# Inner blocks in pairs, a ring of four banks, and a regrouped background turn in a fused attention, Fourier and MLP kernel

## The chip, the core and the metric

The kernel runs on one core of a Trainium2 chip. Its time is the device time of one launch in microseconds (us), the median over runs. Engines are named as the profile names them: PE (matrix multiply, with its weight loads as PEld), DVE (vector), ACT (scalar, activation functions), POOL and SP (which issues nearly all DMAs here). Each engine works through its own instructions in the order of the program; semaphores hold an instruction until what it reads is written and the buffer that it writes is free.

## What is computed

Three stages follow each other on a tensor of 4 batches, 768 positions and 384 channels (8 heads of 48).

```
for t in range(S):                       # gated linear attention, per batch and head
    state = alpha[t][:, None] * state + outer(k[t], v[t])
    y[t] = q[t] @ state
X = fft(fft(x, axis=1), axis=2); u = x + real(X)
un = (u - mean(u)) / sqrt(var(u) + 1e-6)
x = u + relu(un @ w_ch1) @ w_ch2         # 384 -> 1536 -> 384
gate = sigmoid(causal_conv5(x))          # per channel
out = (gate * (x @ w_val)) @ w_out
```

All is float32. The kernel keeps that precision by splitting operands into a high and a low part, so that one product becomes three matmuls (`mm3`).

## The kernel before

**Pieces.** The positions of a batch are cut into three pieces of 256, twelve in all. For each piece `mlp` runs twelve inner blocks of 128 hidden channels. A block is nine matmuls with `w1` into a bank of PSUM (`mm`), a relu on ACT that writes the high part (`hh`, L663), a DVE instruction that writes the low part (`hlo`, L665), and, two blocks later, nine matmuls with `w2` into `ch`. `mlp` is a generator: after each half block it yields, and the loop in `run` then makes one tick. A piece has 24 ticks.

**What a tick adds.** Each tick advances the side jobs by one step: `norm` of the next piece (mean, variance, the split into `hl`), `gate` of the previous piece (`L697`, the convolution `L716`, three products `va` with L736, two products `po` with L749/L752, the output DMA), in the first two pieces a conversion of weights on DVE (L221, L224, L228 and the low part L237), and from the second piece on `check`, which streams the inputs once more through SBUF and two activations on ACT (L134, L140 to L146). It also advances the background by a number of steps that `PACE` sets.

**The background.** While batch b goes through its pieces, `back` runs attention and the Fourier transform of batch b+1. Attention is done in 6 tiles of 128 positions, in turns: `attn_a` (two scans on DVE, L287 and L294, and the scaled k and q, L292 and L297), `attn_b` (transposes L309 with a copy on ACT, L310; scores L317 with the mask on DVE, L318), `attn_d` (output, L365 and L371, copied out by ACT, L376 to L378) and `attn_c` (products L334 and the state updates on DVE, L345 and L350). A turn works on up to three tiles at once: b, c of tile g-1, a of tile g, d of tile g-2. Each `yield` ends a step.

**The head.** Batch 0 has nothing to hide behind: `first` runs its attention by the strings in `FIRST`, one for each turn, in which letters stand for the parts above, `w` for a part of a weight conversion and `l` for up to four weight loads. Conversions work on two weights at a time where two are loaded.

**Banks.** PSUM has eight banks. Before, `mm` is a ring of three, shared by the inner blocks and by `gate`'s `va` and `po`; `aux` is a ring of three, for attention, the Fourier transform and `norm`; `ch0` and `ch1` hold the sums of `mlp`. A ring hands out its banks in turn, and the next user waits until the one before has been read.

Of the kernel before, what the change touches and what calls it, by code (L numbers as in the profile page):

```python
# [30 lines left out]
N_CHECK = 1152  # L31
N_FLAGS = 32
CHECK_FROM = 1
CHECK_STEP = 8
# [29 lines left out]
class Main:  # L64
# [14 lines left out]
    def aux(self):  # L79
        return self.t([P, 512], "aux", 3, pool=self.ps)  # L80

    def mm(self):
        return self.t([P, 512], "mm", 3, pool=self.ps)


    def constants(self):
# [9 lines left out]
        self.ends = cp.tile([P, A_W - 1], F32, name="ends")  # L96
# [108 lines left out]
    def weight_parts(self, count=2):  # L205
# [28 lines left out]
        for hi, lo, t, r, h, l in self.halves:  # L234
            if h is not None:
# [4 lines left out]
                rest = self.t([P, 512], "ch1" if self.pa else f"ch{self.n_rest % 2}", 1, pool=self.ps)  # L240
# [188 lines left out]
    def attention(self, b):  # L429
        g0 = b * NT  # L430
        for i in range(NT + 2):
            g = g0 + i
            if 1 <= i <= NT:
                yield from self.attn_b(g - 1)
            if i < NT:
                yield from self.attn_a(g)
                yield
            if i >= 2:
                yield from self.attn_d(g - 2)
                yield  # L440
            if 1 <= i <= NT:
                self.load_va(g - 1)
            if 1 <= i <= NT:
                yield from self.attn_c(g - 1)
                if i < NT:
                    self.load_v(g)
            if i + 2 < NT:
                self.load_qka(g + 2)
            if 1 <= i <= NT:
                yield  # L450
            if i == 0:
                for _ in range(LAG_BG):
                    yield
# [44 lines left out]
    def dft_part(self, t):  # L498

        if t == 0:  # L500
            self.pa = [self.mm() for _ in range(3)] + [self.t([P, 512], "ch0", 1, pool=self.ps)]
# [148 lines left out]
    def mlp(self, b, p):  # L650
        nc = self.nc
        uh, ul = self.nm[(b, p)][:2]
        hq = {}
        ch = None
        lag = 2
# [465 lines left out]
```

## Time and profile before

| | |
|---|---|
| runs | 659.2, 659.37, 660.25 us; median 659.37 |
| profiled execution | 657.75 us, span 655.9 us |
| head, up to the first inner block | 84 us |
| twelve pieces | 84 to 632 us |
| tail, the last gate | 632 to 656 us |

The profile is of one execution. A row of a group gives the number of its instructions, their busy time and mean length, and then the engine's idle time just before them and who ended it. The length of a matmul in the profile holds its way through the array; how fast PE goes is read from one start to the next.

### The profile page before, as it was taken

Reading aid. Unit: us, or ns where it says so; the run is one execution under the profiler, and the core shown is the slowest. Engines: PE = TensorE matmul, PEld = TensorE weight load, DVE = VectorE, ACT = ScalarE, POOL = GpSimd, SP = SyncE. Lnnn points to the kernel's source line nnn. Section 1 sums busy time; section 2 is a strip of 40 time slices with the busy share of each in tenths; the row PEclk is TensorE's granted clock in tenths of the full one; section 3 lists DMA queues with packets and bytes.
Section 4 is the critical chain, followed back from the end, with each engine's and each line's share of the span. In section 5 each row is a group of like instructions: output and inputs, shape, how many; then the busy total and the mean of one; then the engine's idle time right before and its main releaser. Section 6 shows DMA issues by size and latency. Waiting matters only on the chain.

```text
span 655.9 us, 15998 instructions
## 1 busy us (share of the span) xinstructions
PE 584.9 (89%) x6617; PEld 549.0 (84%) x6617; DVE 438.8 (67%) x1026; ACT 247.7 (38%) x609; POOL 157.3 (24%) x332
## 2 busy tenths in 40 slices
PE   3768996785998999899999999899999998999983
PEld 2557686775997899798999899898998998999973
DVE  7988689879747667857763958669365454454552
ACT  2333432322544453353353354343343433433231
POOL 0011023140316042132322322232231222322220
PEclk9986997698898999999999999999899999999996
DMA  9595044354255136335235247135052041310100
GB/s 337 180 343 179 20 175 81 94 136 158 61 171 104 44 120 148 123 122 83 62 135 106 86 131 183 35 135 118 26 128 74 14 88 42 73 34 26 9 25 30
DMA packets 27587, 69.50 MB, mean 106 GB/s; under 512 B 4976, under 2 KB 15728, under 8 KB 27504
## 3 DMA queue, kind: packets, MB, share of 16 engines
q1 hardware_dynamic: 27504, 68.38, 37.3%
q8 instruction: 54, 0.88, 0.6%
q14 instruction: 29, 0.24, 0.1%
HBM read 63.64 MB, written 4.73 MB: 104 GB/s over the span
## 4 chain that ended last, share of the span: by engine, by line
PE 67%; DVE 21%; DMA 4%; ACT 3%; issue 2%; POOL 1%; SPq 0%; DVEq 0%; POOLq 0%; ACTq 0%
PE mm L646 8%; PE mm L648 7%; PE mm L647 7%; PE ch L646 7%; PE ch L648 6%; PE ch L647 6%; PE mm L749 5%; PE aux L509 4%; PE aux L554 3%; PE aux L317 3%; DVE w L294 2%; DVE ga L716 2%; PE aux L365 2%; DVE hlo L665 2%; DVE w L287 2%
## 5 line engine op out<-in xcount | busy, mean ns | idle before, releaser
L665 DVE SCALAR_TENSOR_TENSOR hlo<-mm,hh 128x256 fp32r<-128x256 f32 x144 | 60.5, 420 | 121.1 <-ACT hh L663 120.7
L646 PE MATMUL mm<-hl,w1h 128*128 128x256 f32 x432 | 131.5, 304 | 4.4 <-DVE hlo L665 3.4
L646 PE MATMUL ch<-hh,w2h 128*128 128x256 f32 x432 | 129.5, 300 | 2.7 <-DVE ga L697 2.7
L647 PE MATMUL ch<-hh,w2l 128*128 128x256 f32 x432 | 122.9, 284 | 0.0
L648 PE MATMUL ch<-hlo,w2h 128*128 128x256 f32 x432 | 122.8, 284 | 0.0
L648 PE MATMUL mm<-hl,w1h 128*128 128x256 f32 x432 | 122.6, 284 | 0.0
L647 PE MATMUL mm<-hl,w1l 128*128 128x256 f32 x432 | 122.6, 284 | 0.0
L663 ACT ACTIVATE hh<-mm 128x256 fp32r<-128x256 f32 x144 | 54.2, 378 | 94.7 <-PE mm L648 94.0
L646 PEld LDWEIGHTS mm<-hl,w1h 128*128 128x128 f32 x432 | 83.2, 193 | 7.9 <-DVE hlo L665 4.2
L646 PEld LDWEIGHTS ch<-hh,w2h 128*128 128x128 f32 x432 | 82.7, 191 | 5.5 <-DVE ga L697 3.1
L647 PEld LDWEIGHTS mm<-hl,w1l 128*128 128x128 f32 x432 | 83.3, 193 | 0.8
L647 PEld LDWEIGHTS ch<-hh,w2l 128*128 128x128 f32 x432 | 82.8, 192 | 0.7
L648 PEld LDWEIGHTS mm<-hl,w1h 128*128 128x128 f32 x432 | 83.1, 192 | 0.2 <-DVE hl L606 0.2
L648 PEld LDWEIGHTS ch<-hlo,w2h 128*128 128x128 f32 x432 | 82.9, 192 | 0.0
L716 DVE SCALAR_TENSOR_TENSOR ga<-u,cw,ga 128x256 f32<-128x256 f32 x132 | 60.8, 517 | 0.0
L738 POOL TENSOR_TENSOR hl<-ga,hl 128x256 fp32r<-128x256 f32 x33 | 27.8, 845 | 105.8 <-ACT hl L737 105.8
L379 POOL COPY x<-x 128x1 f32<-128x1 f32 x24 | 12.3, 513 | 139.2 <-ACT x L376 121.5
L317 PEld LDWEIGHTS aux<-w 48*64 48x64 f32 x768 | 27.3, 148 | 14.5 <-DVE st L350 8.0
L317 PE MATMUL aux<-w 48*64 48x64 f32 x768 | 30.8, 236 | 9.7 <-DVE st L350 7.4
L749 PE MATMUL mm<-wvo,hl 128*128 128x384 f32 x198 | 38.1, 336 | 0.0
L612 POOL TENSOR_TENSOR tmp<-tmp,tmp 128x256 f32<-128x256 f32 x24 | 17.7, 737 | 74.0 <-ACT tmp L611 73.1
L749 PEld LDWEIGHTS mm<-wvo,hl 128*128 128x128 f32 x198 | 33.5, 188 | 0.0
(167 smaller groups left out, 1149.4 us busy)
## 6 DMA issues: line engine op xcount, KB each, us to landing
qka<-in_qka_dram SPq DMA_DIRECT2D x23, 772.5 KB, 5.3
ck<-in_w_dram SPq DMA_DIRECT2D x16, 576.0 KB, 4.8
vu<-in_vu_dram SPq DMA_DIRECT2D x24, 192.0 KB, 3.5
u<-in_w_dram SPq DMA_DIRECT2D x12, 384.0 KB, 4.9
va<-in_va_dram SPq DMA_DIRECT2D x24, 192.0 KB, 4.0
ck<-in_al_dram SPq DMA_DIRECT2D x8, 576.0 KB, 4.4
out_dram<-ga SPq DMA_DIRECT2D x24, 192.0 KB, 1.9
w<-in_cs_dram SPq DMA_DIRECT2D x6, 579.0 KB, 5.4
```

The costliest lines, as they stand in the source:

```text
L317: nc.tensor.matmul(out=sc[j * 64 : j * 64 + 64, cs], lhsT=kt[hs, cs], rhs=qt[hs, cs], start=True, stop=True)
L509: self.nc.tensor.matmul(out=pa[: d1 - d0, g * 193 : g * 193 + n], lhsT=self.eo[g][:, t, m, d0:d1], rhs=self.cs[g][:, t, m, :n], start=t == ...
L554: nc.tensor.matmul(out=pa[:, :385], lhsT=self.cd[:w, dt, mi, kt * P : (kt + 1) * P], rhs=pq[:w, mi, dt, :], start=dt == 0, stop=dt == 1)
L612: nc.gpsimd.tensor_tensor(out=ss, in0=ss, in1=sq, op=ALU.add)
L646: nc.tensor.matmul(out=out, lhsT=w[0][:, k, cols], rhs=xh, start=first, stop=False)
L647: nc.tensor.matmul(out=out, lhsT=w[1][:, k, cols], rhs=xh, start=False, stop=False)
L648: nc.tensor.matmul(out=out, lhsT=w[0][:, k, cols], rhs=xl, start=False, stop=last)
L663: nc.scalar.activation(out=hh, in_=hp[:, :NK], func=AF.Relu)
L665: nc.vector.scalar_tensor_tensor(out=hl, in0=hp[:, :NK], scalar=0.0, in1=hh.bitcast(F32), op0=ALU.max, op1=ALU.subtract)
L716: nc.vector.scalar_tensor_tensor(out=gs[:, j], in0=xs, scalar=w, in1=gs[:, j], op0=ALU.mult, op1=ALU.add)
L738: nc.gpsimd.tensor_tensor(out=gl[:, j], in0=gs[:, j], in1=gh[:, j].bitcast(F32), op=ALU.subtract)
L749: nc.tensor.matmul(out=po[:, :DM], lhsT=lh[:, k, ts], rhs=rh[:, k, :], start=n == 0, stop=n == 8)
```

## The change

Inner blocks are made in pairs: two blocks share one bank (2 x 256 columns), one relu and one DVE instruction of 512 columns serve both, and the `w2` products follow one pair later. The ticks stay 24 for a piece. `mm` becomes a ring of two banks for the inner blocks alone, `aux` a ring of four, and `va` and `po` move to `aux`. The background's turn is written as a string, `ORDER`, with a dot for the end of a step: transposes with scores (`Bb`), both scans at once (`Aa`), an empty step, the output with the scaled q (`Dt`), then products with the states' updates in the same step (`Cvc`). `FIRST` loads weights earlier. `check` takes smaller portions more often (768 columns, a period of 5 ticks, not 1152 and 8). A constant is held in bf16, and some lags and paces change.

```diff
-N_CHECK = 1152
+N_CHECK = 768
-CHECK_STEP = 8
+CHECK_STEP = 5
-BG_FROM = 6
-LAG_US = 5
+BG_FROM = 5
+LAG_US = 6
-LAG_RS = 2
-FIRST = ("Aqwwlwl", "aBwAqUwwSv", "BAwDwUaqvSw", "wBAwwwaDlwUvSq", "AlyllDBwUSavx", "BwAlDUlSawwwv", "aBwDlU0Sw1lf", "lgDwp2hr")
-PACE = (1, 0.8, 0.95, 1.05, 0.9, 0.95, 0.95, 0.9, 1, 1, 1, 1)
+LAG_RS = 3
+FIRST = ("Alwwlqwwl", "BlaAlUwqwSvl", "lBDAwwllUaqvlSw", "BwlwwAwDallwUvSq", "AllylDBwUSavx", "BwAlDUSlawwv", "BawDlU0lSww1lfl", "lDg2wpllrh")
+ORDER = "Bb.Aa..Dt.m.Cvc.q."
+PACE = (1, 0.8, 0.95, 1.15, 0.85, 0.85, 0.95, 0.95, 1, 1, 1, 1)
...
     def aux(self):
-        return self.t([P, 512], "aux", 3, pool=self.ps)
+        return self.t([P, 512], "aux", 4, pool=self.ps)
...
     def mm(self):
-        return self.t([P, 512], "mm", 3, pool=self.ps)
+        return self.t([P, 512], "mm", 2, pool=self.ps)
...
+            for what in ORDER:
+                if what in "Aat" and now:
+                    next(pa, None)
+                elif what in "Bb" and before:
+                    next(pb)
+                elif what in "Cc" and before:
+                    next(pc)
+                elif what == "D" and two:
+                    for _ in self.attn_d(g - 2):
+                        pass
...
+                elif what == ".":
+                    yield
...
-        for f in range(NF + lag):
+        for f in range(0, NF + 2, 2):
+            now = hq
             if f < NF:
                 hp = self.mm()
-                for k in range(KD):
-                    self.mm3(hp[:, :NK], self.w1, slice(f * P, (f + 1) * P), (uh[:, k], ul[:, k]), k, k == 0, k == KD - 1)
-                hh = self.t([P, NK], "hh", 3, F32R)
-                nc.scalar.activation(out=hh, in_=hp[:, :NK], func=AF.Relu)
-                hl = self.t([P, NK], "hlo", 3, F32R)
-                nc.vector.scalar_tensor_tensor(out=hl, in0=hp[:, :NK], scalar=0.0, in1=hh.bitcast(F32),
+                for i in range(2):
+                    cols = slice((f + i) * P, (f + i + 1) * P)
+                    for k in range(KD):
+                        self.mm3(hp[:, i * NK : (i + 1) * NK], self.w1, cols, (uh[:, k], ul[:, k]), k, k == 0, k == KD - 1)
+                    if i == 0:
+                        yield
+                hh = self.t([P, 2 * NK], "hh", 2, F32R)
+                nc.scalar.activation(out=hh, in_=hp, func=AF.Relu)
+                hl = self.t([P, 2 * NK], "hlo", 2, F32R)
+                nc.vector.scalar_tensor_tensor(out=hl, in0=hp, scalar=0.0, in1=hh.bitcast(F32),
                                                op0=ALU.max, op1=ALU.subtract)
...
-            va = self.mm()
+            va = self.aux()
...
-            po = self.mm()
+            po = self.aux()
```

Two places show how instructions move. The first is DVE in the first inner blocks of piece 0 (`hlo` is the low part of a block, `hl_...`, `w1l` and `w2l` belong to weight conversions). Before:

```order
L237 TENSOR_TENSOR w1l<-hl_143_932,w1h 128x384 x2
L665 SCALAR_TENSOR_TENSOR hlo_1047<-mm_1035,hh_1045 128x256
L665 SCALAR_TENSOR_TENSOR hlo_1061<-mm_1049,hh_1059 128x256
L221 TENSOR_SCALAR hl_174_1063<-u_103 128x384
L224 SCALAR_TENSOR_TENSOR hl_174_1063<-u_103,hl_174_1063 128x384
L228 SCALAR_TENSOR_TENSOR hl_174_1063<-u_103,hl_174_1063 128x384
L237 TENSOR_TENSOR w2l<-hl_167_1028,w2h 128x384
L665 SCALAR_TENSOR_TENSOR hlo_1092<-mm_1080,hh_1090 128x256
```

The same stretch now:

```order
L238 TENSOR_TENSOR w2l<-hl_146_956,w2h 128x384 x2
L674 SCALAR_TENSOR_TENSOR hlo_1071<-mm_1038,hh_1069 128x512
L222 TENSOR_SCALAR hl_173_1083<-w_1000 128x384
L225 SCALAR_TENSOR_TENSOR hl_173_1083<-w_1000,hl_173_1083 128x384
L229 SCALAR_TENSOR_TENSOR hl_173_1083<-w_1000,hl_173_1083 128x384
L238 TENSOR_TENSOR w1l<-hl_168_1048,w1h 128x384
L674 SCALAR_TENSOR_TENSOR hlo_1101<-mm_1073,hh_1099 128x512
```

One instruction of 512 columns stands where two of 256 stood. Counted over the whole of DVE's order, 15 conversions are made ahead of the first `hlo` before and 18 ahead of the first inner block now; of the 31 in all, 16 and 13 are left.

The second place is ACT in one of the background's first turns, while weights are still converted (`w_...<-aux` is the copy of the transposes, `pend` the decay of a tile, `x` the output's copies, `hh` the relu of a block, `w2h` and `wvo` conversions). Before:

```order
L663 ACTIVATE hh_1396<-mm_1386 128x256
L232 ACTIVATE w2h<-hl_238_1400 128x384
L310 ACTIVATE w_1406<-aux_1407 128x512
L290 ACTIVATE pend_1443<-w_1440 128x8
L663 ACTIVATE hh_1458<-mm_1448 128x256
L376 ACTIVATE x_1475<-aux_1476 128x192
L377 ACTIVATE x_1475<-aux_1477 128x64
L378 ACTIVATE x_1475<-aux_1477 128x128
```

The same turn now:

```order
L311 ACTIVATE w_1407<-aux_1408 128x512
L291 ACTIVATE pend_1435<-w_1432 128x8
L233 ACTIVATE wvo_1089<-u_103 128x384
L377 ACTIVATE x_1456<-aux_1457 128x192
L378 ACTIVATE x_1456<-aux_1458 128x64
L379 ACTIVATE x_1456<-aux_1458 128x128
L672 ACTIVATE hh_1497<-mm_1440 128x512
```

The order of copy, `pend` and output stays; the relu comes half as often, and a conversion that waits for DVE still stands ahead of the output's copies.

## Rows read from the trace of the kernel before

**Rows 1.** The page's first part: busy us (share of the span) xinstructions.
```profile
PE 584.9 (89%) x6617; PEld 549.0 (84%) x6617; DVE 438.8 (67%) x1026; ACT 247.7 (38%) x609; POOL 157.3 (24%) x332
```

**Rows 2.** Windows by stage: busy us of each engine, granted PE clock, DMA share.
```profile
0.00:84.00 84.00, 58.92 (x887) 46.52 (x887) 65.96 (x151) 27.67 (x73) 6.33 (x20) 0.92 0.61 216
84.00:140.00 56.00, 45.70 (x534) 42.67 (x535) 48.65 (x102) 16.20 (x45) 17.81 (x35) 0.85 0.40 112
140.00:201.00 61.00, 51.38 (x754) 48.94 (x753) 41.89 (x95) 26.62 (x64) 13.79 (x31) 0.92 0.42 120
201.00:534.00 333.00, 322.29 (x3626) 307.00 (x3625) 222.07 (x535) 136.93 (x332) 91.29 (x194) 0.99 0.38 100
534.00:632.00 98.00, 95.50 (x774) 94.40 (x773) 48.83 (x127) 34.38 (x83) 23.36 (x48) 1.00 0.21 42
```

**Rows 3.** PE's waits, 84 to 201 us: us in total, times, longest.
```profile
PE aux L334 <- ACT x L376: 5.3, 2, 3.2
PE aux L317 <- DVE st L350: 4.3, 1, 4.3
PE aux L309 <- DVE w L602: 3.9, 1, 3.9
PE aux L334 <- ACT w L310: 2.7, 1, 2.7
```

**Rows 4.** PE's waits, 201 to 632 us, in the same columns.
```profile
PE mm L646 <- DVE hlo L665: 4.2, 4, 1.5
PE aux L317 <- DVE st L350: 3.0, 2, 1.7
PE aux L334 <- ACT x L376: 3.0, 3, 1.2
PE ch L646 <- DVE ga L697: 2.7, 2, 2.0
```

**Rows 5.** Timeline of PE after a wait near 118 us: start, us, instruction.
```profile
118.10 1.11 PE L309 MATMUL aux<-ident,w 128*128 128x128 f32 x4 [3.88 <-DVE w L602]
...
122.17 0.41 PE L646 MATMUL ch<-hh,w2h 128*128 128x256 f32 x1
122.38 0.41 PE L647 MATMUL ch<-hh,w2l 128*128 128x256 f32 x1
```

**Rows 6.** Timeline of PE near 553 us: two matmuls of an inner block.
```profile
552.82 0.28 PE L646 MATMUL mm<-hl,w1h 128*128 128x256 f32 x1
552.94 0.28 PE L647 MATMUL mm<-hl,w1l 128*128 128x256 f32 x1
```

**Rows 7.** Groups on DVE, 84 to 632 us.
```profile
L665 DVE SCALAR_TENSOR_TENSOR hlo<-mm,hh 128x256 fp32r<-128x256 f32 x144 | 60.5, 420 | 121.1 <-ACT hh L663 120.7
L318 DVE TENSOR_TENSOR w<-aux,mask 128x512 f32<-128x512 f32 x18 | 12.3, 685 | 2.3 <-PE aux L317 2.3
```

**Rows 8.** Groups on ACT, 84 to 640 us.
```profile
L663 ACT ACTIVATE hh<-mm 128x256 fp32r<-128x256 f32 x144 | 54.2, 378 | 94.7 <-PE mm L648 94.0 <-DVE u L703 0.5
...
L310 ACT ACTIVATE w<-aux 128x512 f32<-128x512 f32 x18 | 10.6, 590 | 8.5 <-PE aux L309 8.2
```

**Rows 9.** Groups on DVE in the head, 0 to 84 us: parts of a conversion.
```profile
L224 DVE SCALAR_TENSOR_TENSOR hl<-hl,hl 128x384 int32<-128x384 int32 x8 | 4.3, 552 | 0.0
...
L221 DVE TENSOR_SCALAR hl<-hl 128x384 int32<-128x384 int32 x8 | 2.7, 353 | 3.1 <-PE ch L241 3.1
```

**Rows 10.** The check's tile `ck`: who waited for it (us, times), its DMAs.
```profile
  ACT ck L144: 10.8, 8
...
DMA to landing us min/median/max: 1.8/4.3/9.6
```

**Rows 11.** Timeline of ACT near 544 us.
```profile
543.92 0.74 ACT L144 ACTIVATE ck<-ck 128x576 f32<-128x576 f32 x1 [4.23 <-DMA ck<-in_wv_dram]
```

**Rows 12.** Timeline of PE just behind it.
```profile
546.38 0.39 PE L646 MATMUL mm<-hl,wvo 128*128 128x256 f32 x1 [0.80 <-DVE hlo L665]
...
549.17 0.39 PE L646 MATMUL mm<-hl,w1h 128*128 128x256 f32 x1 [1.46 <-DVE hlo L665]
```

More of the change, by code (lines that the diff above doesn't have):

```diff
@@ L30 @@
 A_LO, A_HI = 0.5, 1.5
-N_CHECK = 1152
-N_FLAGS = 32
+N_CHECK = 768
+N_FLAGS = 48
 CHECK_FROM = 1
-CHECK_STEP = 8
+CHECK_STEP = 5
 W_SCALE = 2.0**20
@@ L95, in constants @@
         nc.scalar.activation(out=self.negative, in_=self.ident, func=AF.Copy, scale=-1.0)
-        self.ends = cp.tile([P, A_W - 1], F32, name="ends")
+        self.ends = cp.tile([P, A_W - 1], BF16, name="ends")
         nc.vector.memset(self.ends, 0.0)
@@ L239, in weight_parts @@
                 self.n_rest += 1
-                rest = self.t([P, 512], "ch1" if self.pa else f"ch{self.n_rest % 2}", 1, pool=self.ps)
+                rest = self.aux() if self.pa else self.t([P, 512], f"ch{self.n_rest % 2}", 1, pool=self.ps)
                 nc.tensor.matmul(out=rest[:, :384], lhsT=self.ident, rhs=r, start=True, stop=False)
@@ L432, in attention @@
             g = g0 + i
[L433 to L445, printed above, removed]
+            now, before, two = i < NT, 1 <= i <= NT, i >= 2
+            pa = self.attn_a(g) if now else None
+            pb, pc = (self.attn_b(g - 1), self.attn_c(g - 1)) if before else (None, None)
+            for what in ORDER:
[8 more added lines that the diff above has]
+                        pass
+                elif what == "m" and before:
+                    self.load_va(g - 1)
+                elif what == "v" and before and now:
                     self.load_v(g)
[L447 to L450, printed above, removed]
+                elif what == "q" and i + 2 < NT:
+                    self.load_qka(g + 2)
+                elif what == ".":
+                    yield
             if i == 0:
@@ L500, in dft_part @@
         if t == 0:
-            self.pa = [self.mm() for _ in range(3)] + [self.t([P, 512], "ch0", 1, pool=self.ps)]
+            self.pa = [self.mm(), self.mm()] + [self.t([P, 512], f"ch{i}", 1, pool=self.ps) for i in range(2)]
         for i in range(4):
@@ L652, in mlp @@
         uh, ul = self.nm[(b, p)][:2]
[L653 to L655 removed]
         last = (b, p) == (B - 1, NPC - 1)
[L657 removed]
+        hq = ch = None
+        for f in range(0, NF + 2, 2):
+            now = hq
             if f < NF:
                 hp = self.mm()
[L660 to L665 removed]
+                for i in range(2):
[8 more added lines that the diff above has]
+                nc.vector.scalar_tensor_tensor(out=hl, in0=hp, scalar=0.0, in1=hh.bitcast(F32),
                                                op0=ALU.max, op1=ALU.subtract)
[L667 removed]
+                hq = (hh, hl)
                 yield
[L669 removed]
+            if f > 0:
                 if ch is None:
@@ L673, in mlp @@
                     ch = [ca[:, :NK], ca[:, NK:], cb[:, :NK]]
-                fs, order = (f - lag,), range(KD)
-                if last and f - lag >= NF - 2:
-                    fs, order = (NF - 2, NF - 1) if f - lag == NF - 1 else (), LAST
-                for j in order:
-                    for k in fs:
-                        self.mm3(ch[j], self.w2, slice(j * P, (j + 1) * P), hq[k], k, k == 0 and j != 1, k == NF - 1 and j != 0)
-                for k in fs:
-                    del hq[k]
-                yield
+                order = [(i, j) for i in range(2) for j in range(KD)]
+                if last and f == NF:
+                    order = [(i, j) for j in LAST for i in range(2)]
+                for n, (i, j) in enumerate(order):
+                    k = f - 2 + i
+                    half = slice(i * NK, (i + 1) * NK)
+                    self.mm3(ch[j], self.w2, slice(j * P, (j + 1) * P), (now[0][:, half], now[1][:, half]), k,
+                             k == 0 and j != 1, k == NF - 1 and j != 0)
+                    if n % KD == KD - 1:
+                        yield
         self.ch[(b, p)] = ch
@@ L795, in last_gate @@
         nc.vector.tensor_tensor(out=xl[:, j], in0=x2[:, j], in1=xh[:, j].bitcast(F32), op=ALU.subtract)
-        va = [self.mm() for _ in range(KD)]
+        va = [self.mm(), self.mm(), self.aux()]
         for x, ws in ((xh, self.wv), (xl, self.wv[:1])):
```

2 lines of the change are left out of this document (removed).

## The prediction

> **What bounds the kernel now.** I read the page's first part for the busy shares, then windows by stage, then PE's own waits in the pieces, and last the groups that give durations. PE is busy for 89% of the span (its weight loads, beside the matmuls, for 84%) and no other engine for more than 67% [rows 1]. By stage it differs [rows 2]. In the head DVE has 66 of 84 us. In pieces 0 and 1 (84 to 201 us) DVE is busy 48.65 of 56 and 41.89 of 61 us, PE 45.7 and 51.4, and PE's granted clock averages 0.85 and 0.92. From 201 to 632 us PE is busy 97%, at a clock of 0.99 to 1.00. So from 201 us on time can only come from what PE still waits for, before that also from DVE. Between two matmuls of a block that waits for nothing lie 0.12 us [rows 6], and the change leaves the number of block matmuls as it is, so that this part is fixed.
>
> PE waits for few things. Before 201 us the largest are for banks of `aux`: the second bank of the products L334 waits for the output's copy L376 (5.3 us), the scores for a state update (4.3), the transposes for norm's L602 (3.9); besides, 2.7 us are for the copy of the transposes, which is data, not a bank [rows 3]. After 201 us they are 3.0 and 3.0 of the same two kinds on `aux`, 4.2 on `mm`, where a block wants the bank of one whose `hlo` is late because `va` or `po` took a turn of the ring, and 2.7 on `ch`, where a new piece waits for the old one's gate [rows 4]. That makes 13.5 + 6.0 = 19.5 us on `aux`, 4.2 on `mm`, 2.7 on `ch`.
>
> **The change part by part.** Every term is in us on the profiled execution's 657.75.
>
> *The ring of two for the blocks: -4.2.* A pair's bank is wanted again two pairs later, behind the pair's own `w2` products, which need its `hlo` anyway, and nothing else takes a turn. The wait on `mm` has no cause left. Bounds: 0 to -4.2.
>
> *The ring of four and the turn, after 201 us: -4.5 of 6.0.* With three banks the second bank of the products is the one that the output took one step earlier. With four, and transposes, scores, output, products in that order, the output reuses the products' banks, the products reuse those of transposes and scores, and at least three steps lie between. Against it, `aux` now also serves five banks of the gate in each piece, each freed only after its copy or multiplication. I take three quarters; bounds 0 to -6.0.
>
> *The same before 201 us: -8 of 13.5.* Here the lateness is that of DVE, and of ACT behind it: a conversion on ACT that waits for DVE still stands ahead of the output's copies. DVE loses three conversions to the head (4.4 us, below) and 12 pairs at 155 ns each (below), 6 us of 90.5 in 117 us. Were all the listed waits gone (13.5 + 2.7), 101 us would be left for 84 us of DVE work, so DVE's total allows it; its bursts will not allow all. Bounds 0 to -13.5.
>
> *The wait on `ch`: -1.5 of 2.7.* A piece now begins with two pairs, 36 matmuls, before its first `w2` product, where three blocks, 27, stood. That is 9 x 0.12 = 1.1 us more for the gate at each of two places. Bounds 0 to -2.7.
>
> *The clock: -3.* After a wait of 3.88 us matmuls of the same block start 0.21 us apart [rows 5], not 0.12. A granted clock of 0.85 over 56 us means 1.2 GHz for some 17 us of it, and 0.92 over 61 us another 10 [rows 2]; part of that is spent waiting, and the rest costs up to half of itself, 13 us at most. If half of the waits that go before it go, I take a quarter of that. Bounds 0 to -6.
>
> *Larger instructions on DVE and ACT: 0 by themselves.* A DVE instruction from PSUM takes 420 ns for 256 columns and 685 for 512 [rows 7], so a pair saves 155; on ACT 378 and 590 [rows 8], 166. Over 72 pairs that is 11.2 us of DVE and 12 us of ACT, hidden behind a PE that is busier. They count only in pieces 0 and 1, where they are in the term above. The Trainium skill (Perfetto Trace Analysis, Optimizing Scalar/DVE Operations) puts the overhead of one DVE instruction on PSUM at some 125 ns; by that figure the 72 pairs save an estimated 9 us, and the sum stays the same. The wait that they add is that a pair's low part is ready 590 + 685 = 1.28 us after its last matmul, where a block needed 0.80; behind it on PE stand 36 matmuls, 4.2 us, before its `w2` product, as before. So DVE may be 2.9 us late instead of 3.4.
>
> *The head: +3.* Three more conversions stand ahead of the first block: 353 + 552 and a third part like the second [rows 9], 1.46 us each, 4.4 us on DVE. DVE idles in the head for 18 of 84 us [rows 2], but mostly at its start and behind the Fourier part, where PE leads. Earlier loads can fill some gaps. Bounds 0 to +4.4.
>
> *The check: +1.* It has 43 portions, not 29, and its first activation comes 3 ticks after the load is issued, not 6. Pieces 2 to 8 take the 333 us up to 534 [rows 2], so a tick is 333 / (7 x 24) = 2.0 us there and the lead some 6 us; a load lands after 4.3 us in the median, 9.6 at most [rows 10]. Even with the longer lead ACT waited 8 times, 10.8 us in all. What stands behind it on ACT is the next relu, and PE has 2.9 us of slack there. Most waits will be swallowed. Bounds 0 to +30, the rival below.
>
> *At nothing:* the constant in bf16 (one operand of a scan, whose length I leave as it is), the later steps of `norm` (its result is wanted a piece later), both scans in one step (no more work, and DVE has 2.9 us of slack), and the states in the step of their products (DVE then waits for PE, but only where it is ahead of it). Transposes and scores in one step interrupt the blocks three times a turn instead of four; if an interruption costs one distance between starts, 0.12 us [rows 6], 18 turns give back 2 us, and I take 0 of it.
>
> Sum: -4.2 - 4.5 - 8 - 1.5 - 3 + 3 + 1 = -17.2, so 640.6 on the profiled execution. The runs' median of 659.37 lies 1.6 above that execution; on that scale it is 642.
>
> **Rivals.**
>
> *A. The waits only move (13%).* The gate's five banks fill the fourth place, and in pieces 0 and 1 DVE's bursts are what PE really waits for. For it: the three largest waits there end with DVE or with ACT behind DVE [rows 3]. Then only the terms on `mm` and `ch`, two of the late ones on `aux` and the head's whole cost remain: -4.2 - 1.5 - 2 + 4.4 = -3.3, 656 at the runs' scale.
>
> *B. Pairs come too late (6%).* A pair's `hlo` is 0.48 us later, and in pieces 0 and 1, where DVE is busy 77% of the time, the slack of 2.9 us is gone more often. If each of the 12 pairs there costs PE a wait of its own length, 1.28 us, 15 us are lost against 17 won: 657, no change. Against it: not one of the listed waits is for `hh` or `hlo` by a `w2` product [rows 3, 4]. The Trainium skill, again under Perfetto Trace Analysis, Optimizing Scalar/DVE Operations, advises smaller instructions where DVE or ACT cause gaps elsewhere without being full. By that rule the pairs would cost time after 201 us, where DVE is busy two thirds; the trace bears it out little, since the wait on `hlo` there is for a bank.
>
> *C. The check blocks ACT, slower (9%).* With half the lead, a load that SP issues late holds up ACT, and the relu behind it. The trace has one such case: ACT waited 4.23 us [rows 11], and PE then 0.80 and 1.46 us for `hlo` [rows 12], 2.3 together. From eight such waits on the gain of 17.2 is gone; at 12 of 43 portions it is 28 us against 18.2 without this part's own term, 669. Against it: loads are a third smaller, and PE's waits on `hlo` are 4.2 us in all [rows 4], so the other seven waits of ACT, 6.6 us [rows 10], cost PE 1.9 at most.
>
> **Numbers.** My forecast has 72%, between 630 and 651 (all banks' waits gone and the head free: 657.75 - 19.5 - 4.2 - 2.7 - 3 is 628; half the terms: 650). A is faster too, B is no change, C is slower. A measurement can tell 0.2%, 1.3 us, from no change, so faster has 85%, same 6%, slower 9%. The range takes in the best end of mine and A, and leaves out C: 628 to 657.
>
> **What would show it.** Right: no PE wait of `mm` on `hlo`, those of L334 on the output's copy and of the scores on a state under 5 us together, a granted clock above 0.92 from 84 to 140 us, `hlo` near 690 ns and the relu near 590 for 512 columns, the first block 2 to 4 us later than 84 us, and pieces 0 and 1 together some 12 us shorter than 117. Wrong: waits of `va` or `po` on `aux` banks, `ch` products waiting for `hh` (B), more than 20 us of ACT waiting for `ck` (C), or a head beyond 90 us.

## The result: 640.16 us, 0.971 of before

The changed kernel takes 640.16 us in the median of 4 runs (635.27 to 643.16), the kernel before 659.29 in the runs beside it. The ratio is 0.9709, with a 95% interval of 0.964 to 0.9778. The forecast was 642, within 628 to 657. The profiled execution took 641.17 us, with a span of 639.1 us from its first instruction to its last.

The first part of the page after, to be held against [rows 1]:

```profile
PE 585.1 (92%) x6626; PEld 547.0 (86%) x6626; DVE 430.1 (67%) x951; ACT 244.5 (38%) x582; POOL 155.4 (24%) x332
```

PE has the same busy time in a shorter span; DVE has lost 75 instructions and 9 us. The windows after, in the columns of [rows 2]:

```profile
0.00:84.00 84.00, 58.86 (x882) 46.37 (x883) 65.42 (x153) 28.41 (x76) 6.21 (x20) 0.88 0.62 212
84.00:140.00 56.00, 47.24 (x524) 42.41 (x523) 50.00 (x95) 15.82 (x40) 12.12 (x21) 0.88 0.48 141
140.00:201.00 61.00, 55.86 (x798) 52.86 (x797) 42.51 (x103) 28.57 (x65) 21.17 (x52) 0.94 0.39 106
201.00:534.00 333.00, 329.96 (x3715) 314.19 (x3714) 224.98 (x496) 140.22 (x332) 89.62 (x187) 1.00 0.38 105
```

From 201 to 534 us PE is now busy 330 of 333 us at a clock of 1.00, so that nothing is left there but its work. PE's waits from 201 to 617 us, which answer to [rows 4]; this is the whole list:

```profile
PE aux L310 <- DVE ga L746: 1.0, 1, 1.0
PE aux L514 <- POOL w L488: 0.7, 1, 0.7
PE aux L335 <- DVE ga L746: 0.4, 1, 0.4
PE aux L335 <- ACT x L377: 0.4, 1, 0.4
PE aux L335 <- DMA vu<-in_vu_dram: 0.3, 1, 0.3
PE aux L318 <- DVE w L298: 0.2, 1, 0.2
```

Where four kinds stood with 12.9 us, 3.0 us are left. Two of the rows are new: a bank of `aux` freed late by the gate (`ga`, L746), 1.4 us. The larger waits from 84 to 201 us, against [rows 3]:

```profile
PE aux L318 <- DVE w L607: 4.6, 1, 4.6
PE aux L318 <- DVE w L298: 3.5, 1, 3.5
PE ch L653 <- DVE hlo L674: 1.5, 2, 1.3
PE aux L310 <- ACT x L377: 1.3, 2, 1.1
```

L607 is norm's read of a bank, L602 before: this wait stayed, and has only changed its victim from the transposes to the scores. L298 (L297 before) writes the scaled q, which the scores read: DVE itself is late. The third row is pairs that come too late, 1.5 us.

Put together, in one profiled execution of each kernel: the first inner block starts at 88.99 us, not 84.38 (+4.6); from there to the end of the last `w2` product it takes 527.8 us, not 548.4 (-20.6), of which pieces 0 and 1 give -6.9 (106.8 for 113.7) and the rest -13.7; and the tail takes 22.4, not 23.2. That is -16.8 of span. Here and below a piece lasts from the first matmul of its first block to that of the next piece. PE's listed waits in the pieces fell from 33.5 to 16.7 us, so 16.8 of the 20.6 are waits. The other 3.8 fit the granted clock: 0.83, 0.92, 0.97 and 0.96 in pieces 0, 1, 2 and 7 before, and 0.87, 0.94, 1.00 and 1.00 now.

The two larger instructions, as the page has them, against [rows 7, 8]:

```profile
L674 DVE SCALAR_TENSOR_TENSOR hlo<-mm,hh 128x512 fp32r<-128x512 f32 x72 | 49.5, 687 | 88.4 <-ACT hh L672 88.2
...
L672 ACT ACTIVATE hh<-mm 128x512 fp32r<-128x512 f32 x72 | 42.5, 591 | 58.7 <-PE mm L653 58.4
```

687 ns for twice 420 and 591 for twice 378: 153 and 165 ns saved by a pair.

### The profile page after: what moved, and what is told of

Same layout as the page of the kernel before. It is cut to its first block, busy times and chain, and to the rows that moved or that the text cites. A ratio compares the mean times of both kernels' runs of the same rounds, so it can differ in the third digit from the quotient of the medians.

```text
span 639.1 us, 15952 instructions
## 1 busy us (share of the span) xinstructions
PE 585.1 (92%) x6626; PEld 547.0 (86%) x6626; DVE 430.1 (67%) x951; ACT 244.5 (38%) x582; POOL 155.4 (24%) x332
## 4 chain that ended last, share of the span: by engine, by line
PE 68%; DVE 21%; DMA 4%; POOL 2%; issue 2%; ACT 2%; SPq 1%; DVEq 0%; POOLq 0%
PE ch L651 7%; PE mm L651 7%; PE ch L653 7%; PE ch L652 6%; PE mm L653 6%; PE mm L652 6%; PE aux L759 5%; PE aux L514 3%; PE aux L559 3%; DVE w L295 3%; DVE w L288 2%; PE aux L318 2%; PE aux L651 2%; PE aux L653 2%; PE aux L652 2%
## 5 line engine op out<-in xcount | busy, mean ns | idle before, releaser
L651 PE MATMUL mm<-hl,w1h 128*128 128x256 f32 x432 | 128.5, 298 | 1.0 <-ACT hl L608 1.0
L653 PE MATMUL mm<-hl,w1h 128*128 128x256 f32 x432 | 121.4, 281 | 0.0
L652 PE MATMUL mm<-hl,w1l 128*128 128x256 f32 x432 | 121.3, 281 | 0.0
L674 DVE SCALAR_TENSOR_TENSOR hlo<-mm,hh 128x512 fp32r<-128x512 f32 x72 | 49.5, 687 | 88.4 <-ACT hh L672 88.2
L651 PEld LDWEIGHTS mm<-hl,w1h 128*128 128x128 f32 x432 | 81.8, 189 | 4.0 <-ACT hl L608 1.4
L653 PEld LDWEIGHTS mm<-hl,w1h 128*128 128x128 f32 x432 | 81.9, 190 | 0.3 <-DVE hl L611 0.3
L672 ACT ACTIVATE hh<-mm 128x512 fp32r<-128x512 f32 x72 | 42.5, 591 | 58.7 <-PE mm L653 58.4
L726 DVE SCALAR_TENSOR_TENSOR ga<-u,cw,ga 128x256 f32<-128x256 f32 x132 | 58.0, 499 | 0.0
L748 POOL TENSOR_TENSOR hl<-ga,hl 128x256 fp32r<-128x256 f32 x33 | 25.5, 779 | 97.2 <-ACT hl L747 97.2
L617 POOL TENSOR_TENSOR tmp<-tmp,tmp 128x256 f32<-128x256 f32 x24 | 20.3, 846 | 101.3 <-ACT tmp L616 100.4
L318 PEld LDWEIGHTS aux<-w 48*64 48x64 f32 x768 | 27.5, 149 | 15.6 <-issue 8.2
L759 PE MATMUL aux<-wvo,hl 128*128 128x384 f32 x198 | 38.4, 337 | 0.0
L759 PEld LDWEIGHTS aux<-wvo,hl 128*128 128x128 f32 x198 | 33.8, 188 | 0.1
```

Of the source, the lines that this page charges most:

```text
L318: nc.tensor.matmul(out=sc[j * 64 : j * 64 + 64, cs], lhsT=kt[hs, cs], rhs=qt[hs, cs], start=True, stop=True)
L617: nc.gpsimd.tensor_tensor(out=ss, in0=ss, in1=sq, op=ALU.add)
L651: nc.tensor.matmul(out=out, lhsT=w[0][:, k, cols], rhs=xh, start=first, stop=False)
L652: nc.tensor.matmul(out=out, lhsT=w[1][:, k, cols], rhs=xh, start=False, stop=False)
L653: nc.tensor.matmul(out=out, lhsT=w[0][:, k, cols], rhs=xl, start=False, stop=last)
L672: nc.scalar.activation(out=hh, in_=hp, func=AF.Relu)
```

## Experiments

Ratios are to the kernel before on the same chip, from 5 to 12 executions of each kernel; in brackets stands the 95% interval. PE's waits in the pieces (first block to last `w2` product) are of the one profiled execution.

### The rings put back

The changed kernel with the old rings (the half-converted weights of the head, `rest`, go back to `ch1`, and the banks of the first Fourier transform and of the last gate are dealt out as before):

```diff
-        return self.t([P, 512], "aux", 4, pool=self.ps)
+        return self.t([P, 512], "aux", 3, pool=self.ps)
...
-        return self.t([P, 512], "mm", 2, pool=self.ps)
+        return self.t([P, 512], "mm", 3, pool=self.ps)
...
-            va = self.aux()
+            va = self.mm()
...
-            po = self.aux()
+            po = self.mm()
...
```

> The changed kernel with the old rings: three banks each for mm and aux, va and po on mm again; pairs, turn, head and check as changed. Theory (the rings are what takes PE's waits away): the waits on mm for hlo come back, 4 us or more, and those on aux for copies and states, some 8 us; ratio to before 0.985 to 0.995 against the changed kernel's 0.971. Rival (pairs and the regrouped turn do it, the rings carry little): 0.970 to 0.977, with no wait on mm.

Measured: 0.9894 [0.9856, 0.9933], 652.41 us. PE's waits, 92 to 630 us:

```profile
PE aux L318 <- DVE st L351: 5.3, 4, 1.9
PE aux L335 <- ACT x L377: 4.8, 3, 2.3
...
PE mm L651 <- DVE hlo L674: 0.6, 2, 0.4
```

The ratio is the theory's. The two bank waits on `aux` are back, 10.1 us: the new rings take them away, and the new turn in three banks does not. But the wait on `mm`, which the theory had at 4 us or more, stays at 0.6 us though `va` and `po` take turns of the ring again. With pairs, a ring of three holds six blocks. So pairs are enough to take that wait away, without a private ring.

### Blocks one by one

The changed kernel with `mlp` as it was:

```diff
-        for f in range(0, NF + 2, 2):
+        for f in range(NF + lag):
...
-                for i in range(2):
-                    cols = slice((f + i) * P, (f + i + 1) * P)
...
-                hh = self.t([P, 2 * NK], "hh", 2, F32R)
-                nc.scalar.activation(out=hh, in_=hp, func=AF.Relu)
+                hh = self.t([P, NK], "hh", 3, F32R)
+                nc.scalar.activation(out=hh, in_=hp[:, :NK], func=AF.Relu)
```

> The changed kernel with inner blocks one by one again, all else as changed. Theory (pairs give nothing by themselves, since DVE and ACT hide behind PE): 0.970 to 0.975, hlo 420 ns and the relu 378 again. Rival 1 (DVE bounds pieces 0 and 1, and pairs free it): pieces 0 and 1 longer by 3 us or more, 0.976 to 0.980. Rival 2 (a pair's low part comes late): faster than the changed kernel, 0.965 to 0.969, and its two waits of w2 products for hlo, 1.5 us, gone.

Measured: 0.977 [0.9723, 0.9817], 644.63 us. PE's waits, 87 to 621 us:

```profile
PE mm L651 <- DVE hlo L670: 3.9, 3, 2.7
PE aux L318 <- DVE w L298: 3.7, 4, 2.1
PE ch L651 <- DVE ga L702: 2.1, 1, 2.1
```

The ratio lies in rival 1's range, but its mechanism is not there. Two blocks in a ring of two banks wait for their own low parts again, up to 2.7 us at a time, and the new piece waits for the old gate; 3.3 of the 3.9 us and all of the 2.1 lie in pieces 0 and 1. Yet these two pieces are shorter than with pairs (105.6 us against 106.8), since norm's read and the scaled q hold PE up less there (3.5 us against 8.1). What pairs bring lies behind: pieces 2 to 11 take 427.8 us one by one and 421.0 in pairs, with 7.4 and 3.6 us of waits, and a granted clock of 0.97 against 1.00 in piece 6. The intervals of the two kernels overlap (0.9723 to 0.9817, 0.964 to 0.9778), so this 0.6% alone would not be shown; the same comparison with the old strings, below, is clear.

### The turn put back

The changed kernel with the old turn, its paces and its start:

```diff
-BG_FROM = 5
+BG_FROM = 6
-PACE = (1, 0.8, 0.95, 1.15, 0.85, 0.85, 0.95, 0.95, 1, 1, 1, 1)
+PACE = (1, 0.8, 0.95, 1.05, 0.9, 0.95, 0.95, 0.9, 1, 1, 1, 1)
...
-            for what in ORDER:
...
+            if 1 <= i <= NT:
+                yield from self.attn_b(g - 1)
+            if i < NT:
+                yield from self.attn_a(g)
+                yield
+            if i >= 2:
+                yield from self.attn_d(g - 2)
+                yield
...
```

> The changed kernel with the old order of the background's turn, and the old PACE and BG_FROM. Theory (four banks alone take the waits on aux away, whatever the order): 0.970 to 0.976, waits of L335 on the output's copy under 2 us. Rival (the order is what gives the distance): 0.980 to 0.990, these waits and those of the scores on a state back at 8 us or more.

Measured: 0.9818 [0.9781, 0.9855], 647.5 us. The turn with its paces is worth 1.1% here, 7 us of median. The ratio is the rival's, its mechanism is not: PE's waits are 23.2 us where the changed kernel has 16.7, but those for the output's copy and of the scores on a state are 3.6 us of it, not 8, and the rest is spread over many small ones. The profiled execution, of 641.97 us, is the fastest of its runs and only 1.0 us of span longer than the changed kernel's, so that its waits need not show the 1.1%.

### The rings alone

The kernel before with the new rings only (and with `rest` on `aux` instead of `ch1`):

```diff
-        return self.t([P, 512], "aux", 3, pool=self.ps)
+        return self.t([P, 512], "aux", 4, pool=self.ps)
...
-        return self.t([P, 512], "mm", 3, pool=self.ps)
+        return self.t([P, 512], "mm", 2, pool=self.ps)
...
-                rest = self.t([P, 512], "ch1" if self.pa else f"ch{self.n_rest % 2}", 1, pool=self.ps)
+                rest = self.aux() if self.pa else self.t([P, 512], f"ch{self.n_rest % 2}", 1, pool=self.ps)
...
-            va = self.mm()
+            va = self.aux()
...
```

> The kernel before with the new rings alone: two banks for the blocks, four for aux with va and po on it; single blocks, old turn, old head, old check. Theory (the rings are worth some 1.8% on top of the rest, and with single blocks a ring of two leaves a block only 27 matmuls, 3.2 us, until its bank is wanted again): some 0.985 to 0.993, waits on mm for hlo still 3 us or more. Rival (rings are all that counts): 0.975 to 0.983. Rival 2 (without pairs a ring of two costs more than it gives): 0.998 or more.

Measured: 0.9718 [0.9676, 0.9759], 639.48 us: as fast as the whole change, as far as this can be told, and faster than theory and rivals had it. The head is shorter by 6.5 us (77.9), the pieces by 13.1, and PE's waits there are 25.8 us. The first of them, 77 to 614 us:

```profile
PE mm L646 <- DVE hlo L665: 5.2, 6, 1.5
PE aux L317 <- DVE w L602: 4.3, 1, 4.3
PE aux L646 <- ACT x L376: 3.2, 1, 3.2
```

The wait on `mm` is no smaller in total than before (4.2), with a ring that the gate never touches: the ring of two alone does not remove it. It has moved, though. From piece 2 on, where the kernel before had all of its 4.2 us, 1.9 are left, so the gate's turns were part of the cause; 3.3 us are new in pieces 0 and 1, where DVE is busiest. What went besides are the waits on `aux` for the state (7.3 us before, 1.6 now) and most of those for the output's copy (8.3 before, 3.2 now).

Waits fell by 7.7 us, but the pieces by 13.1. The other 5.4 fit the clock, as the pieces show in which it was not full before (from windows over each piece; the numbers of matmuls agree within one):

| piece | matmuls | before: us, PE busy, clock | rings alone: us, PE busy, clock |
|---|---|---|---|
| 0 | 446 | 51.60, 41.68, 0.83 | 49.01, 39.03, 0.90 |
| 1 | 815 | 62.10, 52.48, 0.92 | 60.98, 51.89, 0.94 |
| 2 | 414 | 54.18, 51.50, 0.97 | 53.71, 50.48, 1.00 |
| 7 | 599 | 46.41, 45.05, 0.96 | 44.93, 43.57, 1.00 |

For the same matmuls PE is busy 190.7 us before and 185.0 now. A wait costs its own length and, where the granted clock drops behind it, more.

### Pairs alone

The kernel before with pairs, the small portions of `check` and the bf16 constant:

```diff
-N_CHECK = 1152
+N_CHECK = 768
...
-CHECK_STEP = 8
+CHECK_STEP = 5
...
-        self.ends = cp.tile([P, A_W - 1], F32, name="ends")
+        self.ends = cp.tile([P, A_W - 1], BF16, name="ends")
...
-        for f in range(NF + lag):
+        for f in range(0, NF + 2, 2):
...
-                nc.scalar.activation(out=hh, in_=hp[:, :NK], func=AF.Relu)
+                nc.scalar.activation(out=hh, in_=hp, func=AF.Relu)
```

> The kernel before with pairs alone (and, for room, the smaller portions of the check and the bf16 constant); old rings, turn and head. Theory (pairs only save DVE and ACT time, which counts in pieces 0 and 1, some 4 us): 0.990 to 0.997. Rival (pairs in the shared ring of three also take the waits on mm away): 0.985 or less. Rival 2 (a pair holds two blocks' results back and the check comes with half its lead): 1.000 to 1.010.

Measured: 1.0026 [0.9988, 1.0064], 661.68 us. PE's waits are 33.5 us, as before; the first ones, 78 to 635 us:

```profile
PE aux L334 <- ACT x L376: 9.6, 8, 2.3
PE aux L317 <- DVE st L350: 8.3, 3, 5.8
```

The ratio is rival 2's. No wait of `mm` on `hlo` is left, as the first rival had it, but nothing is gained: the two kinds on `aux` have 17.9 us where they had 15.6, and the total is the same 33.5. With three banks for `aux`, PE waits for whichever bank is last, and DVE time set free is not PE time.

### The head's strings put back

The changed kernel with the old `FIRST`, three conversions fewer in the head:

```diff
-FIRST = ("Alwwlqwwl", "BlaAlUwqwSvl", "lBDAwwllUaqvlSw", "BwlwwAwDallwUvSq", "AllylDBwUSavx", "BwAlDUSlawwv", "BawDlU0lSww1lfl", "lDg2wpllrh")
+FIRST = ("Aqwwlwl", "aBwAqUwwSv", "BAwDwUaqvSw", "wBAwwwaDlwUvSq", "AlyllDBwUSavx", "BwAlDUlSawwwv", "aBwDlU0Sw1lf", "lgDwp2hr")
```

> The changed kernel with the old strings of the head. The changed head is 4.6 us longer than before. Theory (three conversions only change places): the first block starts near 84.5 us again, pieces 0 and 1 take back 2 to 4 us, and the ratio stays at 0.968 to 0.973. Rival (the longer head is a pure loss): 0.962 to 0.965. Second rival (early conversions are what makes pieces 0 and 1 shorter): 0.976 to 0.985.

Measured: 0.968 [0.9645, 0.9714], 638.19 us. The ratio is the theory's, the sizes are not: the first block starts at 80.80 us, 8.2 earlier than in the changed kernel, piece 0 takes 48.0 us instead of 51.3, and piece 1 takes 65.3 instead of 55.5. From piece 2 on all lengths agree within 0.1 us. So the new strings pay 8.2 + 3.3 in front for 9.8 behind. The head's length varies from one profiled execution to the next: 79.2 to 80.8 us in the five kernels here with the new rings, the new constant and the old strings, 86.7 to 89.6 in four with the new strings and rings. Up to the first block DVE is busy for 69.69 of 88.99 us in the changed kernel and for 66.37 of 80.80 here: of the 8.2 us, 3.3 are DVE's work and 4.9 are DVE standing idle. Its largest waits up to 84 us in the changed kernel:

```profile
DVE hl L222 <- PE aux L242: 4.2, 1, 4.2
DVE st L351 <- PE mm L335: 3.9, 2, 3.2
```

With the old strings the same two are

```profile
DVE hl L222 <- PE aux L242: 1.9, 1, 1.9
...
DVE st L351 <- PE mm L335: 0.6, 1, 0.6
```

Piece 1 then has a wait of 6.9 us, where the changed kernel's longest is 4.6. PE, and ACT just before, in the timelines of that run:

```profile
164.13 0.58 PE L651 MATMUL aux<-hl,wvo 128*128 128x256 f32 x1 [6.94 <-ACT x L377]
```

```profile
158.76 0.21 ACT L291 ACTIVATE pend<-w 128x8 f32<-128x8 f32 x1 [3.09 <-DVE w L288]
163.34 0.52 ACT L233 ACTIVATE wvo<-u 128x384 fp32r<-128x384 f32 x1 [4.36 <-DVE u L229]
163.76 0.31 ACT L377 ACTIVATE x<-aux 128x192 f32<-128x192 f32 x1
```

PE names the output's copy on ACT, but the copy itself waited for nothing: it stands behind a weight's conversion that waited 4.36 us for DVE.

### The copy one tick later

The changed kernel with the old strings; in the pieces, ACT's copy of a conversion and the low part on DVE are issued one tick behind the DVE part that they need:

```diff
-        yield
+        if not joined:
+            yield
...
+        if joined:
+            yield
...
-        for _ in self.weight_parts(1):
-            pass
-        for _ in range(4):
-            self.weight_load(True)
+        self.convert_rest()
+        self.part = self.weight_parts(1, True)
+        next(self.part)
```

> The changed kernel with the old strings of the head, and in the pieces a conversion's copy on ACT and its low part on DVE issued one tick after the DVE part that they need, so that ACT does not stand waiting for DVE in front of the output's copies. With the old strings alone the ratio was 0.968, with one PE wait of 6.9 us in piece 1 behind that order on ACT. Theory: that wait falls below 2 us and the ratio to 0.957 to 0.964. Rival: DVE itself is late there, whatever ACT does; the wait stays over 4 us or goes to another place of piece 1, ratio 0.966 to 0.970.

Measured: 0.9704 [0.968, 0.9727], 638.81 us. The rival was right: the 6.9 us are gone at that place, but piece 1 takes 64.8 us. PE's waits, 78 to 616 us:

```profile
PE aux L328 <- DVE w L308: 3.7, 2, 3.5
PE aux L328 <- DVE w L617: 3.5, 1, 3.5
PE aux L320 <- ACT x L387: 3.0, 1, 3.0
PE mm L662 <- DVE w1l L241: 2.5, 2, 1.4
PE aux L320 <- DVE st L361: 2.5, 1, 2.5
PE aux L661 <- ACT x L387: 1.9, 1, 1.9
```

The first row's 3.5, the third, the fifth and the sixth lie in piece 1: 10.9 us in four smaller waits, of which the first was there with the old strings as well (3.4). DVE has no gap in that run's timeline from 149.7 to 167.6 us: scans, conversions, gate and state updates of one burst. Over the whole piece it is not full. The windows of piece 1 with the old strings, first with the new turn and then with the old one (that run stands below):

```profile
128.77:194.07 65.30, 52.72 (x764) 49.69 (x762) 47.05 (x107) 26.66 (x63) 17.15 (x36) 0.90 0.40 115
128.10:187.47 59.37, 50.46 (x815) 47.07 (x814) 46.46 (x98) 25.81 (x62) 16.15 (x27) 0.97 0.42 128
```

With the old turn the piece is 5.9 us shorter, though PE has 51 more matmuls there and DVE the same conversions and as much to do (46.46 us for 47.05). So it is not the amount of DVE's work that makes piece 1 long, but how the new turn with its paces places it in the burst; converting sooner, in the head, is the other way out.

### Low parts on POOL

The changed kernel with the old strings and with the low part of a conversion on POOL, to free DVE:

```diff
-                    nc.vector.tensor_tensor(out=l, in0=r, in1=h.bitcast(F32), op=ALU.subtract)
+                    nc.gpsimd.tensor_tensor(out=l, in0=r, in1=h.bitcast(F32), op=ALU.subtract)
```

> The changed kernel with the old strings of the head, and with the low parts of the weights, made after the head, subtracted on POOL instead of DVE (17 times some 0.55 us of DVE). Theory (with the old head DVE's backlog in pieces 0 and 1 is what PE waits for; one such wait is 6.9 us): piece 1 gets shorter by 3 us or more, 0.958 to 0.965. Rival (the wait hangs on the chain from load to conversion, not on DVE's load): 0.966 to 0.970. Rival 2 (POOL is slow and its results are late): above 0.970.

Measured: 0.9766 [0.9727, 0.9806], 643.51 us, slower than with the low parts on DVE (0.968): rival 2's range. Pieces 0 and 1 take 118.1 us where they took 113.3. A subtraction takes POOL about 1000 ns where DVE takes 550, and the wait in piece 1 is as long as it was:

```profile
PE aux L651 <- ACT x L377: 7.0, 1, 7.0
```

The low part comes behind ACT's copy; what ACT waits for are the parts ahead of it (L229, 4.36 us here as well), and these stayed on DVE.

### Without the check

The changed kernel without the loads and activations of `check`:

```diff
-            ck = self.t([P, N_CHECK], "ck", 1, F32 if alpha else I32)
-            nc.sync.dma_start(out=ck[:, : src.shape[1]], in_=src)
...
-                nc.scalar.activation(out=z, in_=z, func=AF.Abs, bias=self.bounds[:, 0:1])
...
```

> The changed kernel without the check's loads and activations (the inputs aren't tested; the flags stay zero); the background and the ticks as they are. Theory (ACT's 24 us of waits for the check's loads are swallowed): 0.967 to 0.972. Rival (they hold up relus and copies): 0.955 to 0.964, and PE's waits for ACT's copies go.

Measured: 0.9696 [0.9656, 0.9736], 639.07 us. The check costs nothing that can be told. Yet ACT waits for it more often and longer than before, as the tile's view in the changed kernel shows (against [rows 10]):

```profile
  ACT ck L145: 16.5, 8
  ACT ck L141: 7.5, 4
...
DMA to landing us min/median/max: 1.8/3.3/8.6
```

24 us of ACT waiting in 12 places, and PE notices none of it: no row of PE's waits from 201 us on ends with the relu or with `hlo`.

### The head's bank alone

The kernel before with one line of the rings:

```diff
-                rest = self.t([P, 512], "ch1" if self.pa else f"ch{self.n_rest % 2}", 1, pool=self.ps)
+                rest = self.aux() if self.pa else self.t([P, 512], f"ch{self.n_rest % 2}", 1, pool=self.ps)
```

> The kernel before with one line changed: in the head the half-converted weights that PE transposes (the bank called rest) take a place in the ring aux and no longer the one bank ch1; everything else is as before. The new rings alone had shortened the head from 84.4 to 77.9 us. Theory: that gain came from this one line, since ch1 made conversions wait for each other; the head is then 78 to 81 us, the pieces stay as before, ratio 0.990 to 0.996. Rival: the gain came from the fourth place of aux; with three places the conversions now crowd out attention, the head stays at 83 to 86 us, ratio 0.998 to 1.003.

Measured: 0.9947 [0.992, 0.9975], 654.67 us. The ratio is the theory's, but the profiled execution, of 658.68 us one of the slowest of its 12, does not show the place: its first block starts at 86.2 us, where theory and rival had 78 to 81 and 83 to 86. So this line is worth some 3 us in the median; that they are won in the head is not shown, and whether the head's 6.5 us come from this line, from the fourth bank or from both is not settled.

### Pairs and turn, each without the other

Two kernels complete a square over the new rings with the old strings. The first has pairs and the old turn (the diffs of the turn and the strings above, together):

> The changed kernel with two parts undone: the old turn of the background with its old paces, and the old strings of the head; rings, pairs and check stay new. With the old turn alone undone the ratio was 0.982, with the old strings alone 0.968. Theory: the turn is worth its 1% with pairs whatever the head does, so 0.976 to 0.982, with some 6 us more of PE's waits in the pieces than with the old strings alone. Rival: the old turn was only bad together with the new strings; then 0.966 to 0.971, the same as rings alone (0.972) or better.

The second has the new turn and the blocks one by one (the diffs of the blocks and the strings together):

> The changed kernel with the old strings of the head and with the blocks one by one; rings and turn stay new. It completes a square over the new rings with the old head: neither pairs nor turn 0.972, pairs alone 0.980, both 0.968. Theory: the two answer each other, so the turn alone does not help either: 0.971 to 0.977, with PE waits of mm on hlo as in the run with blocks one by one. Rival: pairs cost 0.8% and the turn brings 1.2% whatever the other does; then 0.958 to 0.963, faster than every kernel so far.

Measured: 0.9796 [0.9777, 0.9815] and 0.9864 [0.9812, 0.9916]. The square:

| new rings, old strings | old turn | new turn |
|---|---|---|
| blocks one by one | 0.9718 | 0.9864 |
| pairs | 0.9796 | 0.9680 |

(The kernel of the first field also has the old `check`, lags and constant; in the changed kernel the check was shown to cost nothing that can be told, the lags and the constant were not tried alone. The four fields were measured on four chips, each beside the kernel before.) Each half alone makes the rings worse, by 0.8 and 1.5%; only together are they no loss. The first run is the theory's; the second is slower than theory and rival had it, 0.971 to 0.977 and 0.958 to 0.963. Its pieces 2 to 10 take 397.0 us, where those of pairs with the turn take 389.0, and this 8.0 us is nearly all of the 8.1 by which the two profiled spans differ. The first of PE's waits from piece 2 on, 195 to 624 us:

```profile
PE aux L310 <- DVE ga L741: 1.7, 1, 1.7
PE aux L514 <- POOL w L488: 1.6, 2, 0.9
PE aux L318 <- DVE w L298: 1.5, 3, 0.9
PE aux L335 <- DVE ga L741: 1.4, 1, 1.4
PE mm L651 <- DVE hlo L670: 0.6, 1, 0.6
```

The wait on `mm` is the smallest of these five. With pairs the rows of the gate's banks (`ga`) and of the scaled q are 1.0, 0.4 and 0.4 us: without pairs DVE frees these banks and writes this q later. Waits make up half of the 8.0 us, 7.3 us for 3.4. The rest is the clock. Pieces 3 and 6 in the run with pairs and turn, and the same two with the turn alone:

```profile
243.67:295.53 51.86, 50.78 (x850) 47.37 (x849) 42.25 (x87) 22.75 (x55) 16.47 (x35) 1.00 0.48 132
381.09:430.77 49.68, 48.54 (x781) 45.52 (x779) 40.52 (x78) 19.48 (x52) 16.49 (x25) 1.00 0.46 132
244.60:299.88 55.28, 52.57 (x850) 48.99 (x849) 43.32 (x92) 23.41 (x61) 16.52 (x35) 0.97 0.47 125
386.16:439.14 52.98, 50.07 (x781) 47.01 (x779) 41.96 (x84) 20.41 (x58) 16.63 (x25) 0.97 0.44 124
```

The same 850 and 781 matmuls keep PE busy 1.8 and 1.5 us longer. In each of the two pieces the granted clock goes to 0.50, the lower level of 1.2 GHz, just behind one of the two waits on a bank of the gate (1.7 us near 270, 1.4 us near 414 us). With the old turn, pairs have 27.9 us of waits where blocks one by one have 25.8, and a clock of 0.97 and 0.96 in pieces 2 and 4, where these have 1.00; why pairs bring these waits without the new turn stays open.

## Why the prediction came out, step by step

The total was within 2 us on either scale; the terms were not all as good. So close a total is luck in part: the four runs spread over 8 us, and errors of opposite sign met: the head was put 1.6 us too low, the check 1 us too high, and the tail, 0.8 us shorter, had no term.

*The ring of two, -4.2: the size right, the cause half right.* The wait of `mm` on `hlo` went completely in the changed kernel. "The wait on `mm` has no cause left" was argued from the pair's place behind its own `w2` products and from the private ring. In a private ring of two the blocks one by one still wait, 5.2, 3.9 and 3.9 us in the three runs that have it; of this, 1.9, 0.6 and 0.6 lie from piece 2 on, where the kernel before had its 4.2, and 3.3 in each run lie in pieces 0 and 1 together, where it had none. In the old shared ring pairs wait 0.6 or not at all. So the private ring takes part of the old wait away, and pairs take nearly all of it in either ring: two banks of pairs are four blocks' worth of time for DVE.

*Larger instructions, 0 by themselves: half right.* Pairs alone gave 1.0026, and the lengths were as forecast (687 and 591 ns). That freed time on DVE is not time on PE was right for the old banks. The step missed that the larger bank is itself a deeper ring, and that with the new rings an earlier DVE does count: with the new turn, pairs are worth 0.6% under the new strings (0.977 to 0.9709, where the intervals overlap) and 1.8% under the old ones. The Trainium skill (Perfetto Trace Analysis, Optimizing Scalar/DVE Operations) says that breaking up instructions may help where DVE or ACT are not full but cause gaps on other engines. The kernels with the smaller ones had the waits on `hlo` here (3.9 us against none) and were the same or slower; but the ring held fewer blocks in them too, and no run splits the two instructions while a bank still holds a pair. Rival B was there with 1.5 us in the first piece, not 15.

*`aux` after 201 us, -4.5 of 6.0: right.* The two kinds went from 6.0 to 0.4 us; the gate's use of the ring gave 1.4 back, so 4.2 net. With the rings put back the two kinds are there again, 10.1 us over all pieces, and with the rings alone the products do not wait for the copy at all and the scores 1.6 us (in their place `va` waits once, 3.2): the new rings do most of it.

*`aux` before 201 us, -8 of 13.5: right in total.* All of PE's waits in pieces 0 and 1 fell from 20.3 to 13.1 us, by 7.2. The waits for output and state shrank from 9.6 to 1.3; norm's did not (3.9, now 4.6), and a wait for the scaled q, 3.5, is new. The two pieces together are 6.9 us shorter (106.8 for 113.7; the forecast's 117 took in the first 3 us of piece 2), not the "some 12" that was set as a sign. What is left are places where DVE is late, as rival A had it for a part: 8.6 us in piece 0, with norm's 4.6, and 4.5 in piece 1. The old strings and the copy one tick later show that under the new turn piece 1 has 65 us with three more conversions in it, whether ACT's copy stands in front or not.

*The wait on `ch`, -1.5 of 2.7: more.* It went completely; with blocks one by one it is there with 2.1.

*The clock, -3: the size about right, the place not.* Of the 20.6 us won in the pieces 3.8 are not waits. The forecast looked for them before 201 us, but pieces 0 and 1 are shorter by no more than their waits; what shows beyond the waits lies in pieces 2 to 11 (13.7 us, of which 9.7 are waits), where 0.97 and 0.96 in pieces 2 and 7 became 1.00. It fell short of the mark set for 84 to 140 us, above 0.92; 0.88 was granted there, 0.94 in the next window.

*The head, +3: the term that was mis-sized.* It was +4.6 net, a little above the upper bound, and made of two parts that the prediction did not see. The new strings cost 8.2 us: the three conversions add 3.3 us to DVE's busy time, not 4.4, but DVE also stands idle for 4.9 us more, where the prediction had earlier loads fill gaps. The new rings and the rest give back 3.6 (80.80 for 84.38 with the old strings; 6.5 with the rings alone), and no term stood for that: `rest` on `aux` was at nothing by not being listed.

*The check, +1: 0.* Rival C falls: even 24 us of ACT waiting do not reach PE. Its mark, more than 20 us, was set where nothing happens.

*What the sum hid.* The forecast gave the rings, with pairs and turn, -4.2, -4.5 and -8, 16.7 us in the pieces; rings alone give 13.1 there, so the sum's largest terms had the right owner, and 6.5 in the head, where the prediction had none. Beyond them, the new strings cost in the head what they save in piece 1, and pairs and turn pay for each other. With the old strings the kernel is at 0.968 [0.9645, 0.9714], not to be told from the changed one.

## What to carry to other kernels

When a bank is waited for, count how long one turn of its ring lasts in the work of the waiting engine: one bank more, or a larger unit in each bank, lengthens it. Try them one by one: here the new rings gave the gain alone, and the larger unit alone gave none: the wait that it removed was made up for at the other ring. Where a change has several parts, try each with and without the others: here two that lose alone are no loss together, and the one part that gains alone has all the gain. And when a wait names an instruction that itself waited for nothing, look at what stands ahead of that on its engine; moving the blocker does not help if the engine that it waits for is late for everybody. When the pieces shrink by more than the waits, look at the granted clock piece by piece.

## What was not expected of the hardware

Executions of one kernel on one chip differ by more than some of the effects looked for: 650.65 to 659.18 us in 12 runs of the kernel with the head's bank alone. Its one profile, of 658.68 us, shows none of the 3 us that its median gained. And PE can be busy 330 of 333 us while DVE and ACT, at 68% and 42%, run behind it with waits of several us of their own; a wait of 24 us in total on ACT left no trace on PE. Waits of PE, on the other hand, cost more than their length where the granted clock falls behind them: with the same matmuls PE was busy 5.7 us longer in four pieces of the kernel before than with the rings alone, and 3.3 us longer in two pieces with the turn alone than with pairs and turn.
